# Two-operand SBUF instructions ahead of the up projection pinned to GpSimd, and a new instruction order

## The chip, the cores and the metric

The kernel runs on one core of a Trainium2 chip. The metric is device time in microseconds (us): the time before is the median of three runs. In the profile the engines are called PE (TensorE matmul), PEld (TensorE weight load, beside PE), DVE (VectorE), ACT (ScalarE), POOL (GpSimd) and SP (SyncE, which issues nearly all DMAs). Each engine works through its own list of instructions in order; semaphores hold an instruction until what it reads or overwrites is ready.

## The reference

One block of a network on x of 2048 tokens by 512 channels, in fp32, with six modulation rows (silu(c) times w_mod). First half: linear attention with 32 heads of 16 channels; second half: a token-shift mixer and an MLP with 1376 hidden channels.

```python
x = A_x
mod = (_silu(c) @ w_mod).reshape(c.shape[0], 6, 1, -1)
sa, ca, ga, sb, cb, gb = (mod[:, 0], mod[:, 1], mod[:, 2], mod[:, 3], mod[:, 4], mod[:, 5])
h = _layernorm(x, axis=-1) * (1 + ca) + sa
x = x + ga * _A_ref(h, A_wqkv, A_w_phi, A_wo)
h = _layernorm(x, axis=-1) * (1 + cb) + sb
x = x + gb * _B_ref(h, B_w1, B_w2, B_w3, B_w4)

# in _A_ref: per head, phi = (softmax(p), softmax(-p)) of p = q @ w_phi and of p = k @ w_phi
kv = jnp.einsum("bhsf,bhsd->bhfd", phi_k, v)
z  = jnp.einsum("bhsf->bhf", phi_k)
num = jnp.einsum("bhqf,bhfd->bhqd", phi_q, kv)
den = jnp.einsum("bhqf,bhf->bhq", phi_q, z)[..., None] + 1e-6
o = num / den

# in _B_ref: h = gelu(layernorm(x) @ w1), four channel quarters shifted by +1, -1, +2, -2 tokens
x1 = x + hs                                   # hs = shifted h @ w2
h2 = _gelu(_layernorm(x1, axis=-1) @ w3) @ w4  # the up projection is w3, the down projection w4
return x1 + h2
```

## The kernel before

Tokens are worked in 8 chunks of 256 (c) and in 16 tiles of 128 rows (t). A product of two fp32 operands is made of three fp32r matmuls on a high and a low part of each (`three`), so every operand is split: one instruction copies the high part, a second one subtracts it from the source to get the low part (`hi_lo`). That subtraction has two SBUF operands where the source lies in SBUF, and so has most of what this change touches.

The body does not issue instructions. It records about 2800 steps in a plan, each with an engine, the engines that could do it instead (`alts`), and what it reads and writes. At the end `emit` issues them in the order of the table ORDER: a list of step numbers, where a letter behind a number sends the step to another engine that it allows (A is ACT, V is DVE, G is POOL). SLOT gives the buffer of every tile of each kind. Both tables were found ahead of time by a planner that is not in the file. So the place of each instruction on its engine, and its buffer, are fixed numbers.

The stages, by the names of their groups in `plan.at` and of their tiles:

- `wk`, `wq`, `wv`: weights of the first half are folded or split (`bd`, `rk`, `raw`, tile `w`); `w1`, `w2`, `gb`: modulation rows are accumulated (`mod`, `acc`); `w3`: `wo` is scaled by ga and split; `w7`: w1 and w2 are split.
- `h`: layer norm of a chunk (`xl`, `xn`, transposed in `pt`, split into `hh`). `k`: key features `ke` of a tile (reductions `k`, exponentials, then `ke` times the reciprocal sums). `v`: `vv`. `kv`: 32 small matmuls into `kva`, and the sum of the features over tokens, `za`, plus `ke`. `q`: query features `qe`, by way of a copy `qt` for most tiles, and a store to DRAM.
- `phi`: features come back as `e`; `ez` is `e` times the column sums `z` of `za` (broadcast), reduced to the denominators `pz`. `tr`: `e` times the weights `q`, then a DVE transpose to `pT`. `num`: matmuls on `pT`, then `oT`. `o`, `n`: projection by wo, residual, two moments of layer norm (each with a POOL power `rs`), transposed and split to `nT`. `g`: w1, gelu into `gf`, split into `sh`. `sh`: small POOL copies of two columns between the `sh` of neighbouring chunks, for the shifts. `x`: the matmuls by w2 on `sh`.
- `w50` to `w54`: five parts of w3 (`wr`) are made into seven products each (`ws`: sums and differences, then splits) and stored to DRAM, since the up and down projections use a scheme with seven block products. `w40` to `w44`: w4, scaled by gb and split (`raw`, `tw`, `w`).
- `l`, `t`: layer norm of the second half and its block operands (`bL`, `tr`, `bH`). `u`: the up projection (PE tile `pa` from `bH` and the w3 products `wq`). `b`, `d`, `out`: the down projection (`ac` from `gg`) and the output.

Two-operand instructions are recorded by `tt`. Those that may run on DVE or POOL get POOL as an alternative, and ORDER decides for each one. In the profile a tile's trailing digits are cut off, so `k1` and `k2` both read `k`, and `q1` to `q5` read `q`; in the order lists below names end with a running number of the buffer.

Of the kernel before, what the change touches and what calls it, by code (L numbers as in the profile page):

```python
# [164 lines left out]
)  # L165
SLOT = {
    "pp": "510234426360573046405216574732325716511600313075732270653365216523706542035040435752736700267672"
          "4243153510404460571",
    "bd": "46",
    "w": "134625cd387165ad28cb09",  # L170
    "rk": "73958dgc",
# [195 lines left out]
def body(ctx: ExitStack, tc, x, wqk_t, wv_d, wo_d, w1_d, w2_d, w3_d, w4_d, c_d, wmod_d, id_d, cst_d, cst2_d, out):  # L367
# [308 lines left out]
    if BIAS["start"] > 1:  # L676
        plan.at("wq")
        wq = load_folded(0)
# [709 lines left out]
```

## Time and profile before

| | |
|---|---|
| median of 3 runs | 554.66 us (554.64 to 555.55) |
| the profiled execution | 554.69 us, of which the instructions span 552.9 us |
| PE busy | 544.9 us, 4498 matmuls |
| DVE busy | 488.6 us, 903 instructions |
| ACT busy | 351.7 us, 828 instructions |
| POOL busy | 344.5 us, 351 instructions |
| HBM | 89.74 MB read, 34.35 MB written |

How to read it: a view by windows gives the busy time of each engine in stretches of the span. A view of groups gives, for instructions of one line, engine and shape, count, total and mean time, and behind the second bar how long the engine had been idle before them and which engine and line ended most of that. A timeline row merges neighbouring instructions of one kind: start, length, engine, what, how many. The chain of work that ended last is followed back from the last instruction, at each step to what released it.

### The profile page before, as it was taken

Reading aid. Unit: us, or ns where it says so; the run is one execution under the profiler, and the core shown is the slowest. Engines: PE = TensorE matmul, PEld = TensorE weight load, DVE = VectorE, ACT = ScalarE, POOL = GpSimd, SP = SyncE. Lnnn points to the kernel's source line nnn. Section 1 sums busy time; section 2 is a strip of 40 time slices with the busy share of each in tenths; the row PEclk is TensorE's granted clock in tenths of the full one; section 3 lists DMA queues with packets and bytes.
Section 4 is the critical chain, followed back from the end, with each engine's and each line's share of the span. In section 5 each row is a group of like instructions: output and inputs, shape, how many; then the busy total and the mean of one; then the engine's idle time right before and its main releaser. Section 6 shows DMA issues by size and latency. Waiting matters only on the chain.

```text
span 552.9 us, 12370 instructions
## 1 busy us (share of the span) xinstructions
PE 544.9 (99%) x4498; PEld 488.1 (88%) x4498; DVE 488.6 (88%) x903; ACT 351.7 (64%) x828; POOL 344.5 (62%) x351
## 2 busy tenths in 40 slices
PE   8999999999989999999999999999999999999997
PEld 7888788878767788888889898999999999999996
DVE  3999999899999999999998878987888868896886
ACT  2899898834436788969888877866434543434540
POOL 2499985979599999978886545234150434254442
PEclk9999999999999999999999999999999999999999
DMA  8982544537736766869987878986689673872022
GB/s 323 392 277 89 175 170 137 176 112 248 205 118 226 249 195 206 275 235 319 292 275 270 242 257 301 339 356 231 284 248 347 245 284 97 264 286 80 25 92 95
DMA packets 63749, 124.90 MB, mean 226 GB/s; under 512 B 7140, under 2 KB 26852, under 8 KB 59592
## 3 DMA queue, kind: packets, MB, share of 16 engines
q1 hardware_dynamic: 63400, 124.04, 66.4%
q8 instruction: 35, 0.57, 0.4%
q14 instruction: 26, 0.21, 0.1%
q10 hardware_dynamic: 288, 0.07, 0.1%
HBM read 89.74 MB, written 34.35 MB: 224 GB/s over the span
## 4 chain that ended last, share of the span: by engine, by line
PE 86%; DVE 7%; POOL 3%; DMA 2%; issue 1%; ACT 0%; DVEq 0%; POOLq 0%
PE pp L471 36%; PE pa L471 27%; PE ac L471 20%; PE pt L480 2%; DVE pz L442 2%; DVE q L442 2%; DMA mod<-in_wmod 1%; PE kva L471 1%; POOL qe L420 1%; DVE pT L762 1%; POOL ez L420 1%; POOL e L420 1%; DVE ez L418 1%; DMA const<-in_c 1%; DVE pp L437 0%
## 5 line engine op out<-in xcount | busy, mean ns | idle before, releaser
L471 PE MATMUL pp<-w,hh 128*128 128x512 f32 x576 | 138.8, 397 | 0.0
L471 PEld LDWEIGHTS pp<-w,hh 128*128 128x128 f32 x576 | 106.7, 188 | 26.1 <-issue 1.6
L471 PE MATMUL pa<-bH,wq 128*128 128x256 f32 x840 | 106.7, 281 | 0.0
L471 PE MATMUL ac<-w,gg 128*128 128x256 f32 x840 | 106.6, 281 | 0.0
L471 PEld LDWEIGHTS ac<-w,gg 128*128 128x128 f32 x840 | 103.4, 189 | 1.1
L471 PEld LDWEIGHTS pa<-bH,wq 128*128 128x128 f32 x840 | 103.1, 189 | 0.9
L471 PE MATMUL pp<-w,sh 128*128 128x512 f32 x192 | 49.4, 399 | 0.0
L471 PE MATMUL pa<-nT,w 128*128 128x256 f32 x384 | 48.3, 282 | 0.8 <-DVE nT L418 0.7
L471 PEld LDWEIGHTS pa<-nT,w 128*128 128x128 f32 x384 | 46.8, 188 | 2.5 <-DVE nT L418 1.2
L471 PE MATMUL pp<-w,oT 128*128 128x512 f32 x192 | 47.4, 395 | 0.0
L471 PEld LDWEIGHTS pp<-w,oT 128*128 128x128 f32 x192 | 35.4, 188 | 8.1 <-DVE oT L418 0.7
L401 ACT ACTIVATE gg<-cu 128x256 fp32r<-128x256 f32 (+1 forms) x56 | 19.1, 359 | 35.1 <-PE ac L471 19.7
L471 PEld LDWEIGHTS pp<-w,sh 128*128 128x128 f32 x192 | 34.6, 188 | 7.5 <-issue 0.8
L588 POOL TENSOR_TENSOR rs<-mv,const 128x2 f32<-128x2 f32 x31 | 23.8, 769 | 25.3 <-ACT mv L595 23.7
L401 ACT ACTIVATE cu<-pa 128x512 f32<-128x512 f32 (+1 forms) x42 | 21.5, 519 | 27.6 <-PE pa L471 22.3
L420 POOL TENSOR_TENSOR gg<-cu,gg 128x128 fp32r<-128x128 f32 (+1 forms) x26 | 15.8, 615 | 33.2 <-ACT gg L401 13.9
L420 POOL TENSOR_TENSOR ez<-e,const 128x1024 f32<-128x1024 f32 x12 | 29.2, 2433 | 5.2 <-DMA dram<-qe 5.1
L401 ACT ACTIVATE gg<-sg 128x512 fp32r<-128x512 f32 x38 | 23.1, 624 | 14.0 <-POOL sg L420 6.0
L420 POOL TENSOR_TENSOR e<-e,q 128x1024 f32<-128x1024 f32 x15 | 28.8, 1938 | 0.4 <-DVE q L418 0.2
L418 DVE TENSOR_TENSOR gg<-cu,gg 128x256 fp32r<-128x256 f32 (+1 forms) x54 | 22.1, 416 | 7.6 <-PE ac L471 4.6
L418 DVE TENSOR_TENSOR gg<-sg,gg 128x512 fp32r<-128x512 f32 x36 | 26.0, 722 | 3.0 <-PE ac L471 1.5
L420 POOL TENSOR_TENSOR ke<-ke,k 128x1024 f32<-128x1024 f32 x14 | 27.2, 1952 | 1.2 <-DVE k L445 1.2
(214 smaller groups left out, 1211.5 us busy)
## 6 DMA issues: line engine op xcount, KB each, us to landing
wq<-dram SPq DMA_DIRECT2D x32, 1024.0 KB, 7.8
dram<-ws SPq DMA_DIRECT2D x35, 256.0 KB, 3.1
xl<-in_x SPq DMA_DIRECT2D x32, 256.0 KB, 4.1
dram<-qe SPq DMA_DIRECT2D x16, 512.0 KB, 3.7
e<-dram SPq DMA_DIRECT2D x64, 128.0 KB, 3.2
raw<-in_w SPq DMA_DIRECT2D x18, 256.0 KB, 3.7
mod<-in_wmod SPq DMA_DIRECT2D x16, 256.0 KB, 5.2
dram<-xl SPq DMA_DIRECT2D x16, 256.0 KB, 3.0
```

Source lines behind the costliest of these rows:

```text
L401: nc.scalar.activation(o(), i(), func, **kw)
L418: dve = ("DVE", 71 + 1.04 * o.n + 90 * (isps(a) and isps(b)), lambda: nc.vector.tensor_tensor(o(), a(), b(), op=op))
L420: pool = ("Pool", cost, lambda: nc.gpsimd.tensor_tensor(o(), a(), b(), op=op))
L442: plan.op("DVE", 65 + 1.04 * a.n + 110 * isps(o), lambda: nc.vector.tensor_reduce(o(), a(), axis=AX.X, op=op), [o], [a])
L471: nc.tensor.matmul(o(), a(), b(), start=s, stop=e, **kw)
L480: nc.tensor.transpose(o(), i(), ident())
L588: plan.op("Pool", 540 + 10 * m, lambda: nc.gpsimd.tensor_tensor(r(), v(), mhalf[:, :m](), op=OP.pow), [r], [v, mhalf])
L762: plan.op("DVE", 71 + 1.04 * o.n, lambda: nc.vector.transpose(o(), i()), [o], [i])
```

## The change

`tt` looks at the group of a step. In the groups `k`, `q`, `kv`, `w` (with digits: w0 to w7, w50 to w54 and w40, but not w41 to w44), `phi`, `tr`, `g`, `sh` and `gb`, a step that could run on either engine is recorded for POOL alone. Everything with an operand in PSUM stays on DVE, and so do the small instructions that had no alternative. The groups of the up and down projections keep their choice. ORDER and SLOT are replaced as a whole, so all engines run their work in a new order, the choices that are left (copies on ACT, DVE or POOL, and the free two-operand steps) are made anew, and tiles have other buffers. The file is three lines longer in all, and `tt`'s DVE instruction has line 417 in place of 418, its POOL instruction line 419 in place of 420.

```diff
 ORDER = (
-    "0 3 35 6 52 2 42 50 5 54 56 36 237 23 7 37 11 1 12 13 14 17G 31 10 38 86G 19 39 43 88 8 44 18 9 49V 84 27 40 "
...
+    "2744 2786 2702 2666 2785 2758 2667 2787 2668 2774 2700 2760 2788 2759 2789 2791G 2703 2771 2790 2775 2704 "
+    "2792G 2772 2793 2795 2794 2776 2796 2799 2797 2800 2798"
 )
 SLOT = {
...
-    "bd": "46",
+    "bd": "39",
...
         pool = ("Pool", cost, lambda: nc.gpsimd.tensor_tensor(o(), a(), b(), op=op))
         both = lock and (o.n >= 256 or eng != "DVE")
-        plan.op(*dve, [o], [a, b], alts=[pool] if both else [], lock=lock)
+        g = plan.group.rstrip("0123456789")
+        if both and g in ("k", "q", "kv", "w", "phi", "tr", "g", "sh", "gb") and plan.group not in ("w41", "w42", "w43", "w44"):
+            plan.op(*pool, [o], [a, b])
+        else:
+            plan.op(*dve, [o], [a, b], alts=[pool] if both else [], lock=lock)
```

The first place is on DVE, where the denominators of the first query tiles are made (`ez` is e times z, `pz` the reduction). Before:

```order
L418 TENSOR_TENSOR ke_1708<-ke_1708,k_340_1738 128x1024
L418 TENSOR_TENSOR w_1730<-raw_1436,w_1703 128x512
L418 TENSOR_TENSOR qe_1826<-qt_1755,q_345_1762 128x1024
L418 TENSOR_TENSOR w_1671<-raw_1295,w_1271 128x512
L418 TENSOR_TENSOR ez_1902<-e_1388,const_1853 128x1024
L418 TENSOR_TENSOR ez_1906<-e_1618,const_1853 128x1024
L442 TENSOR_REDUCE pz_1925<-ez_1902 128x64
```

and DVE at the same place now:

```order
L445 TENSOR_REDUCE q_343_1789<-qt_1781 128x32 x2
L409 TENSOR_SCALAR vv_1827<-pp_1792 128x512
L409 TENSOR_SCALAR const_1851<-pp_1822 128x256
L445 TENSOR_REDUCE pz_1893<-ez_1884 128x64
L445 TENSOR_REDUCE pz_1893<-ez_1891 128x64
L440 SCALAR_TENSOR_TENSOR pz_1893<-q_313_1530,pz_1893 128x64
```

Six two-operand instructions left DVE here, and two copies out of PSUM (`vv` and the column sums, `const`) came in from ACT.

The second place is POOL in the same part of the program: the last sums of keys, the first `ez`, the first `e`. Before:

```order
L420 TENSOR_TENSOR ke_1680<-ke_1680,k_339_1733 128x1024
L420 TENSOR_TENSOR za_800<-za_800,ke_1680 128x1024
L420 TENSOR_TENSOR ez_1908<-e_1782,const_1853 128x1024
L420 TENSOR_TENSOR w_1671<-raw_969,w_1271 128x512
L1007 MEMSET sh_1955 128x4x2
L420 TENSOR_TENSOR qe_1959<-qt_1910,q_368_1930 128x1024
L420 TENSOR_TENSOR e_1388<-e_1388,q_377_1966 128x1024
L420 TENSOR_TENSOR e_1618<-e_1618,q_377_1966 128x1024
```

and POOL now:

```order
L419 TENSOR_TENSOR za_791<-za_791,ke_1608 128x1024
L419 TENSOR_TENSOR ke_1716<-ke_1716,k_334_1742 128x1024
L419 TENSOR_TENSOR qe_1829<-qt_1781,q_343_1789 128x1024
L419 TENSOR_TENSOR ez_1884<-e_1221,const_1851 128x1024
L419 TENSOR_TENSOR ez_1891<-e_1524,const_1851 128x1024
L419 TENSOR_TENSOR w_1915<-raw_1430,w_1296 128x512
L419 TENSOR_TENSOR ez_1941<-e_1711,const_1851 128x1024
L419 TENSOR_TENSOR e_1221<-e_1221,q_371_1962 128x1024
L419 TENSOR_TENSOR qe_1990<-qt_1939,q_372_1964 128x1024
L419 TENSOR_TENSOR ez_2001<-e_1908,const_1851 128x1024
L419 TENSOR_TENSOR e_1524<-e_1524,q_371_1962 128x1024
```

All four first `ez` are on POOL now, and the second `e` is the 104th instruction of the plan on POOL where it was the 90th.

The third place is POOL at the column copy from the `sh` of chunk 3 into the `sh` of chunk 2 (a CAST, the last of the rows shown); the w2 matmuls of tile 5 (`x5`) read it. Before:

```order
L420 TENSOR_TENSOR sh_3316<-gf_3252,sh_3316 128x2x256
L420 TENSOR_TENSOR ws_3241<-ws_3241 128x256
L420 TENSOR_TENSOR ez_3419<-e_2781,const_1853 128x1024
L588 TENSOR_TENSOR rs_3455<-mv_3416,const_118 128x2
L1004 CAST sh_3085<-sh_3316 128x4x2
```

and now:

```order
L419 TENSOR_TENSOR sh_3355<-gf_3281,sh_3355 128x2x256
L419 TENSOR_TENSOR raw_1966<-raw_1966,gb_2524 128x512
L419 TENSOR_TENSOR w_3490<-raw_3104,w_3308 128x512
L591 TENSOR_TENSOR rs_3503<-mv_3438,const_67 128x2
L419 TENSOR_TENSOR e_2809<-e_2809,q_670_3497 128x1024
L419 TENSOR_TENSOR e_3087<-e_3087,q_670_3497 128x1024
L1007 CAST sh_3566<-sh_3355 128x4x2
L419 TENSOR_TENSOR tw_3571<-raw_1966 128x256
L1007 CAST sh_3238<-sh_3355 128x4x2
```

The copy was the 168th instruction of the plan on POOL and is the 196th now. Counted by kind, up to and with the copy: `za` 9 before and 14 now, `ez` 12 and 16, `ws` 34 and 45, `w` (subtractions of 512) 13 and 16, `raw` 3 and 6, `ke` 14 and 16, `e` 12 and 14, `sh` (subtractions) 6 and 8, `qe` 11 and 12, `acc` (additions) 11 and 12, `tw` 0 and 1; fewer are `acc` (scalings) 3 and 0, `bd` 4 and 2, `xn` 3 and 2, `mod` 2 and 1, `w` (copies) 2 and 1. The copies between chunks are 6 and 7; all other kinds are the same in number.

More of the change, by code (lines that the diff above doesn't have):

```diff
@@ L40 @@
 ORDER = (
[124 rows of a table removed]
[123 rows of a table added]
 )
 SLOT = {
-    "pp": "510234426360573046405216574732325716511600313075732270653365216523706542035040435752736700267672"
-          "4243153510404460571",
-    "bd": "46",
-    "w": "134625cd387165ad28cb09",
-    "rk": "73958dgc",
-    "xl": "01lif20gi5bh89hdfh4a36c0kejafg2h50eh36ecj9hl0aac",
-    "st": "03b8g32eh379c16aej5837hgb7h96dj2b",
-    "mv": "14fa06bdj2bdg379c16c68i2h9ie7064a",
-    "rs": "26hc17fi148hj2bdg34j2a19ef1c4f78e",
-    "nm": "57ei9dj54a89cg056afei0548fhi02bd54bd03aiaeg0fj581cg539hi",
@@ L177 @@
-    "xn": "ab75aj6ejag7f54b",
-    "mod": "ekbk73e1dj930hf2ke",
-    "mod2": "1023",
-    "kva": "4",
-    "za": "7",
-    "hh": "0789abe0",
-    "pt": "71713064136760724740255030200105",
-    "raw": "948hcla7b2l2g59fd34940abi351",
-    "k1": "0110502430210140",
-    "ke": "4501639451823940",
-    "k2": "5343025543253140",
-    "vv": "3246ekjhkfh0170l",
-    "qe": "7692282134682731",
-    "q1": "3242123515032015",
-    "qt": "ajj9ib759209",
-    "acc": "clf1e",
-    "kvs": "1",
-    "pz": "1",
@@ L195 @@
-    "q2": "03105351",
-    "e": "5617956458034928",
-    "ez": "4988322399990775",
-    "q3": "1245243214024032",
-    "q5": "44423145",
-    "pT": "3044399695373795",
-    "oT": "4a4ea04b",
-    "nT": "b05444be",
-    "n": "l12l4aaf1h5kje7g",
-    "h": "7519l62c7i1lfkcd",
-    "gf": "21535500",
-    "sh": "92be2cb0",
-    "pa": "720435033552357536277143075740636220453477601263027041460272",
-    "wr": "80061",
-    "ws": "010ie23c3782d1hgibgibgfbd0id69267k7",
-    "gb": "8",
-    "tw": "08935",
@@ L212 @@
-    "bL": "47604149",
-    "nb": "dgdj5dhj4gg4jbjd",
-    "yt": "9fje7gehj940707c",
-    "bH": "23820419431994595628147378657521",
-    "tr": "e10a2k3haldgbhd0",
-    "wq": "e90c934e174e3174e7314e7134e14317e431",
-    "cu": "672egi14hdfl25b7c1364hg9ked6l14g9cd0jblf",
-    "gl": "big235l6",
-    "ac": "26311637061227465013415304762351",
-    "gg": "25789138572584716831287609283795063284107962583265103241806937415809261809713458",
-    "sg": "kf6fka6k0j0k94h3la253c4b4acl7276ki2k97e4",
-    "xb": "9had9ei0fj3haf15",
@@ L224 @@
-    "xc": "5le904k6jhi2fg2i",
-    "uu": "00k2i6ck",
+    "pp": "261305532640421075722365757064416403320062054043536071021151535323725140237431473401270212137314"
+          "1455126707426232736",
+    "bd": "39",
+    "w": "124635ce7812d93eab4c61",
+    "rk": "6548agfd",
+    "xl": "01jk728f34250h629fjklc4b12fjf94005bejea995bfkik2",
+    "st": "04b8i57ah56fh12cej4653hd88e95i128",
+    "mv": "15fa03cej27ei56fh12d26iah9ge4jd7c",
+    "rs": "26gc16fg1acbj37di5a1ac09ehjf7g46e",
+    "nm": "37dh9ej4289dbi04389dg04a89bg037f478g13cbcbi0bj26f053a9hb",
@@ new lines @@
+    "xn": "bc530h2e8j1diflj",
+    "mod": "e41kbb6l7j0g1gcdfb",
+    "mod2": "0123",
+    "kva": "7",
+    "za": "6",
+    "hh": "0789abd0",
+    "pt": "17061432046516324014155271147117",
+    "raw": "adei5bec5ea38ilg9i4chl3g82j3",
+    "k1": "0115103053403512",
+    "ke": "4510832450897120",
+    "k2": "0245412514230503",
+    "vv": "jlagakic2kc0bk60",
+    "qe": "8692987557041279",
+    "q1": "3243210425301425",
+    "qt": "6c4dh60hdg4d",
+    "acc": "i9bl1",
+    "kvs": "k",
+    "pz": "6",
@@ new lines @@
+    "q2": "01431415",
+    "e": "3492856084157839",
+    "ez": "6166611591981242",
+    "q3": "2352052052302340",
+    "q5": "44310235",
+    "pT": "0666519698212482",
+    "oT": "94a04a4b",
+    "nT": "6b5645cb",
+    "n": "a0a0jajl6961f5cf",
+    "h": "h86eckda28kb61a0",
+    "gf": "73451854",
+    "sh": "93b5abc6",
+    "pa": "020450207004503750163642753457216043701622754731536201453626",
+    "wr": "71360",
+    "ws": "7c9dkh4f45h6905d30e36bhld39g5e4j81g",
+    "gb": "7",
+    "tw": "59618",
@@ new lines @@
+    "bL": "73075863",
+    "nb": "l9h5dii0ckki8lel",
+    "yt": "0f00ef59h9lh6dld",
+    "bH": "41597429841261092637406918177164",
+    "tr": "dh4lhajdiac08gj6",
+    "wq": "406407580278502785207850278027580752",
+    "cu": "edc3b4915hc8a6jhf3dik8cilba9f02gi384jh60",
+    "gl": "gb5e3c2g",
+    "ac": "02615612745373620147041723054172",
+    "gg": "65341526939852493682794617093417289350487215970297524906825790132485017235906481",
+    "sg": "6g60ai0g524le21de50ed65k8j0hfa9l5fag5lbf",
+    "xb": "f50k9bg241kde61k",
@@ L226 @@
+    "xc": "ejgelc4a1d0350ac",
+    "uu": "h45669i0",
 }
```

244 rows, old and new, of the table ORDER are left out of this document.

## Prediction

> **What bounds the kernel now.** I read the page first: the busy times, the slices and the chain that ended last.
>
> ```profile
> span 552.9 us, 12370 instructions
> ...
> PE 544.9 (99%) x4498; PEld 488.1 (88%) x4498; DVE 488.6 (88%) x903; ACT 351.7 (64%) x828; POOL 344.5 (62%) x351
> ...
> PE   8999999999989999999999999999999999999997
> ...
> POOL 2499985979599999978886545234150434254442
> ...
> PE 86%; DVE 7%; POOL 3%; DMA 2%; issue 1%; ACT 0%; DVEq 0%; POOLq 0%
> ```
>
> PE sets the time: it is idle for 8 us of the span, and four fifths of the chain are its matmuls. The change moves no matmul to or from PE, so it can help by little, and can hurt where another engine makes PE wait. POOL's 62% hide two halves: slices of 7 to 9 up to about 280 us, mostly 2 to 5 later. The edit puts work into the full half. So I went to windows, cut where the argument needs it.
>
> ```profile
> core 0: us, PE busy (x) PEld busy (x) DVE busy (x) ACT busy (x) POOL busy (x), PEclk, DMA share, GB/s
> 0.00:60.00 60.00, 58.30 (x340) 49.14 (x340) 50.23 (x90) 45.21 (x109) 41.34 (x46) 1.00 0.74 266
> 60.00:150.00 90.00, 90.00 (x864) 72.12 (x864) 86.12 (x112) 58.99 (x128) 71.06 (x46) 1.00 0.53 170
> 150.00:259.00 109.00, 106.48 (x954) 87.98 (x953) 106.62 (x180) 79.87 (x186) 100.48 (x81) 1.00 0.70 224
> 259.00:300.00 41.00, 41.00 (x367) 35.79 (x365) 39.51 (x68) 34.46 (x91) 34.27 (x37) 1.00 0.84 278
> ```
>
> Up to 259 us POOL works 41.34 + 71.06 + 100.48 = 212.9 us and idles 46.1: 18.7 in the first window, 18.9 in the second, 8.5 in the third. DVE is as full: 243 of 259.
>
> I cut at 259 because there POOL makes the column copy between the shifted tiles of chunks 2 and 3, which the w2 matmuls of tile 5 need (third place in the order lists).
>
> ```profile
> 259.04 0.19 POOL L1004 CAST sh<-sh 128x8 fp32r<-128x8 f32 x1
> 264.35 4.37 PE L471 MATMUL pp<-w,sh 128*128 128x512 f32 x18
> ```
>
> The copy ends at 259.2. PE's row of 18 matmuls holds tile 6 and tile 5 mixed, three matmuls a part; the first part that reads the copy starts about 0.5 us into it. In the new PE order some 1.3 us of other matmuls come ahead of it, so PE would reach it at about 266. Slack: about 7 us. I tried the same subtraction at earlier points (last `ke` for the sums, first `e`, the fourth chunk's) and it comes out later and later as POOL's list goes on; this copy is where it is worst.
>
> **The change, part by part.**
>
> *Work put on POOL ahead of the copy.* Counts are from the order lists, durations from these groups:
>
> ```profile
> ...
> L420 POOL TENSOR_TENSOR za<-za,ke 128x1024 f32<-128x1024 f32 x8 | 19.3, 2413 | 4.3 <-DVE za L418 4.3
> L420 POOL TENSOR_TENSOR ez<-e,const 128x1024 f32<-128x1024 f32 x12 | 29.2, 2433 | 5.2 <-DMA dram<-qe 5.1
> L420 POOL TENSOR_TENSOR ws<-ws 128x256 fp32r<-128x256 f32 x14 | 10.5, 756 | 4.0 <-ACT ws L401 3.9
> L420 POOL TENSOR_TENSOR w<-raw,w 128x512 fp32r<-128x512 f32 x13 | 17.9, 1375 | 0.1
> L420 POOL TENSOR_TENSOR raw<-raw,acc 128x512 f32<-128x512 f32 x2 | 2.6, 1288 | 0.0
> L420 POOL TENSOR_TENSOR ke<-ke,k 128x1024 f32<-128x1024 f32 x14 | 27.2, 1952 | 1.2 <-DVE k L445 1.2
> L420 POOL TENSOR_TENSOR e<-e,q 128x1024 f32<-128x1024 f32 x15 | 28.8, 1938 | 0.4 <-DVE q L418 0.2
> L420 POOL TENSOR_TENSOR sh<-gf,sh 128x512 fp32r<-128x512 f32 x11 | 12.2, 1121 | 3.8 <-DVE sh L410 3.6 <-ACT nm L595 0.2
> L420 POOL TENSOR_TENSOR qe<-qt,q 128x1024 f32<-128x1024 f32 x11 | 22.4, 2036 | 3.3 <-DVE pz L437 2.5 <-DVE q L442 0.8
> L410 POOL TENSOR_SCALAR acc<-mod,const 128x512 f32<-128x512 f32 x3 | 2.1, 696 | 0.8 <-ACT xn L401 0.8
> L420 POOL TENSOR_TENSOR bd<-const 128x128 f32<-128x128 f32 x4 | 1.7, 454 | 4.5 <-DMA const<-in_cst 4.5
> ```
>
> Added: 5 `za` 12.1; 4 `ez` 9.7; 11 `ws` at 0.75, 8.2; 3 `w` 4.1; 3 `raw` and 1 `acc`, of the same size, 5.2; 2 `ke` 3.9; 2 `e` 3.9; 2 `sh` 2.2; 1 `qe` 2.0; 1 `tw`, 256 wide as `ws`, 0.8. Together 52.1 us. Gone: 3 scalings of `acc` 2.1; 2 `bd` 0.9; three copies of 512 elements like the scalings, 2.1. Net: 47 us, so POOL has 212.9 + 47 = 260 us of work up to the copy.
>
> *How much idle time stays.* Were there none, the copy would end at 260. The idle time of the first 60 us is waiting for loads and the first features:
>
> ```profile
> POOL w L410 <- DMA raw<-in_wv: 7.8, 1, 7.8
> POOL bd L420 <- DMA const<-in_cst: 4.5, 1, 4.5
> POOL za L420 <- DVE za L418: 4.3, 2, 2.6
> POOL ez L420 <- DMA dram<-qe: 5.1, 1, 5.1
> POOL rs L588 <- ACT mv L595: 9.0, 5, 3.2
> PE pp L471 <- DVE pT L762: 1.7, 1, 1.7
> ```
>
> The first two are of that kind, and DVE and PE have the same work up to there, so I keep 18.7 and add one for the first `qe`, which has less POOL work ahead of it now: 20. The next two are POOL out of work, waiting for its turn in a sum that DVE shared, or for the first reloaded features. With `za` all its own and a backlog of tens of us these go. The ends are none of the 27.4 us after 60 us, and half of it (the `rs` row, waits on moments from ACT, may recur in any order). I take none: from the thirteenth slice to the seventeenth (166 to 235 us), where POOL had a backlog before too, its slices read 9.
>
> *The sum.* 260 + 20 = 280 us for the copy, against 266 for PE: 14 late. In the overlap with DVE, POOL's rows get longer:
>
> ```profile
> 145.46 2.82 POOL L420 TENSOR_TENSOR ez<-e,const 128x1024 f32<-128x1024 f32 x1 [5.13 <-DMA dram<-qe]
> 148.24 2.30 POOL L420 TENSOR_TENSOR w<-raw,w 128x512 fp32r<-128x512 f32 x1
> 255.66 2.40 POOL L420 TENSOR_TENSOR ez<-e,const 128x1024 f32<-128x1024 f32 x1
> 31.91 1.28 POOL L420 TENSOR_TENSOR w<-raw,w 128x512 fp32r<-128x512 f32 x1
> 145.95 3.42 DVE ez L418
> ```
>
> The same `ez` and `w` took 2.82 and 2.30 beside DVE's two `ez` (3.42), 2.40 and 1.28 elsewhere: 1.4 us more. DVE's `ez` are gone, so I take 1 off: 13 late. Were all of POOL's 260 us 2% shorter for lack of such company, it would be 5 off, 9 late; without the us for the first `qe`, 8: the lower end. The upper end, with half of the later idle time kept, is 28.
>
> The Trainium skill, in Advanced Engine Details and Errata, VectorE Performance Modes, says that DVE's second SBUF port is shared with GpSimd and that two-port DVE instructions and GpSimd block each other. By that rule the edit takes away one side of the quarrel, and the sum would be 9 late, 564 us, where the group means give 13 and 568. The five rows agree with it.
>
> The wait builds up rather than falling on one matmul: the column sums need the last `ke`, then the first `num` the second `e` (104th on POOL, 90th before), then the shifts. Behind each, PE's whole list is queued. After the copy POOL's list goes on at a pace below PE's (34.27 of 41 us busy before), so the distance closes. I keep 13 us to the end, since nothing on PE can be made up: 58.3 of 60, 90 of 90, 41 of 41.
>
> *What else moves.* DVE loses about as many instructions of 0.7 to 1.8 us as POOL gains, some 34 us, and takes about 20 copies out of PSUM from ACT, 14 us: free, since PE waits for POOL then. SP's list carries the stores of `ws` in their new places; the last that counts for the up projection's third product is 43 POOL instructions, 38 us, behind the copy: 280 + 38 = 318, then
>
> ```profile
> dram<-ws SPq DMA_DIRECT2D x35, 256.0 KB, 3.1
> wq<-dram SPq DMA_DIRECT2D x32, 1024.0 KB, 7.8
> ```
>
> so 329 us. By its place in PE's list of matmuls, PE comes to that product at about 330 without delay and 343 with it: hidden, with some 13 us over; if SP were held up longer than that, the rest would be added one for one. The start (PE waits for the same loads) and the tail (down projection, not pinned) I cost at nothing, within 1 us each way. The profiled execution is 554.69 us, its span 552.9, the median of the runs 554.66. So 552.9 + 13 = 566 for the span and 554.7 + 13 = **568 us** for the time.
>
> **Rivals.**
>
> *POOL's cover holds, no change* (553.6 to 555.7). POOL had 46.1 us idle before the copy and gets 47; with all of it used and 7 us of slack, PE would not wait. Against it: 18.7 of the idle us lie where there is nothing to do yet. It decides at 13 us of 260, that is POOL 5% faster than its rows; no group above has that much to give.
>
> *DVE was the brake, faster.* The chain runs through DVE and POOL for much of 144 to 204 us, and PE loses time there:
>
> ```profile
> 154.00:168.00 14.00, 12.28 (x131) 9.37 (x120) 13.86 (x21) 6.05 (x12) 13.90 (x8) 1.00 0.41 132
> ```
>
> With two `ez` and other work off DVE, the 1.7 us of PE idle (the wait for `pT` above) could go: 554.7 - 1.7 = 553. It decides if POOL has the `e` for that `pT` done by then; but POOL is busy 13.90 of 14 here, as full as DVE, with more work ahead of that `e` now.
>
> *POOL waits too, much slower.* PE, held up by POOL, hands `o` and `n` to POOL's powers (`rs`) later, and POOL's list is in order, so it stands behind them with the `ez` of later tiles: the two engines then wait in turns. Half of 27.4 us of idle time comes back: 554.7 + 28 = 583 at the end, 576 to 590. For it: 9.0 us of waits of `rs` on ACT before; against it, they were where POOL had run dry.
>
> *The clock.* The 1.7 us above are PE's longest idle time between 12 and 549 us, and the clock stayed full.
>
> ```profile
> 549.00:551.00 2.00, 0.08 (x1) 0.00 (x0) 0.75 (x2) 0.00 (x0) 0.00 (x0) 1.00 0.55 183
> 551.00:552.90 1.90, 0.00 (x0) 0.00 (x0) 0.00 (x0) 0.00 (x0) 0.00 (x0) 0.57 0.18 65
> ```
>
> At the end it falls to 0.57 two us after the last matmul. If the 13 us come as three or four waits of over 2 us, each could be followed by a slow stretch, a microsecond or two; most of that would be taken out of the next wait for POOL, and only behind the last does it count: 570. TensorE: Matmul & The Clock Gate, Part 1, of the Trainium skill, puts the idle window and the time to recover at about 3.4 us each, half clock between; by it one such wait costs an estimated 1.7 us, the same 570.
>
> **How the numbers follow.** Two kernels are told apart from about 0.2%, 1.1 us. POOL sets the pace and PE ends 8 to 21 us late: 0.70, 562 to 576, likeliest 568; in 0.15 of this the clock falls behind the last wait (570). Less than 8 but over 1.1 us: 0.08. Waiting in turns, over 576: 0.14. No change 0.03, faster 0.05. So slower 0.92. From 560 to 579 there lies the first case, about half of the second and a third of the third: 0.8.
>
> **What would show it.** Right: POOL's slices read 9 from the third to about the twentieth; its busy time goes from 344 to about 390 us; PE idle, in waits of some us between 140 and 270 us, put down to POOL's `ke`, `e` or `sh` or DVE's `pT` behind them; POOL's share of the chain far above 3%; the copy at about 280; DVE's busy time lower and its idle time larger; from 300 us on all as before. Wrong: POOL idle for more than 25 us up to the copy (in turns), POOL's means shorter by 4% or more (the cover holds), or PE's waits put down to loads by SP.

## Result and the profile after

The changed kernel takes 564.98 us (median of four runs, 564.34 to 565.49), the kernel before beside it 554.88 us: 1.018 times as long, 95% interval 1.0167 to 1.0194. That is 10 us slower. The profiled execution took 564.34 us.

First the page of the changed kernel: the busy times, POOL's slices and the chain that ended last.

```profile
span 562.6 us, 12352 instructions
...
PE 549.2 (98%) x4498; PEld 488.0 (87%) x4498; DVE 478.1 (85%) x896; ACT 341.9 (61%) x811; POOL 379.9 (68%) x375
...
POOL 1499999999999999999997844625140323423422
...
PE 58%; DVE 2%; issue 0%; DVEq 0%
```

POOL gained 35 us, DVE lost 10.5 and ACT 10. POOL's slices are full from the third to the twenty-first, as the forecast had it. The chain shows no POOL, but its shares add up to only 60%: its first piece starts at 218.3 us, so it is silent on all that came earlier. The same windows as before:

```profile
0.00:60.00 60.00, 58.13 (x342) 47.77 (x342) 51.52 (x92) 46.81 (x110) 39.37 (x41) 1.00 0.78 280
60.00:150.00 90.00, 88.97 (x856) 71.24 (x853) 74.58 (x102) 52.16 (x116) 90.00 (x61) 1.00 0.44 140
150.00:259.00 109.00, 103.13 (x921) 83.56 (x920) 99.66 (x165) 71.73 (x163) 109.00 (x85) 0.98 0.72 221
259.00:300.00 41.00, 41.00 (x332) 33.71 (x331) 37.84 (x67) 33.72 (x91) 38.74 (x40) 1.00 0.85 280
```

POOL idles for 20.6 us in the first window and then not once up to 259 us. PE is full again from 259 on: what it loses, it loses before, most of it in the third window (5.9 idle there against 2.5 before). The column copy of the forecast and PE's rows around it:

```profile
274.65 0.21 POOL L1007 CAST sh<-sh 128x8 fp32r<-128x8 f32 x1
```

```profile
274.80 0.67 PE L474 MATMUL pp<-pT,const 64*32 64x128 f32 x32
275.39 2.36 PE L474 MATMUL pp<-w,sh 128*128 128x512 f32 x9
```

The copy ends at 274.9, and the parts that need it start at 275.39, close behind, yet in an unbroken run of matmuls. So nothing is waited for there. PE's longest waits, from the list of waits:

```profile
PE pa L474 <- ACT nT L400: 2.1, 1, 2.1
PE pp L474 <- DVE pT L765: 1.7, 1, 1.7
PE pp L474 <- POOL ke L419: 1.0, 1, 1.0
```

The wait for `pT` is the one of before; the other two are new. How late PE is at a place is read from rows of the same matmuls. Ahead of the last three places PE has done the same matmuls in both kernels; ahead of the first the changed kernel has done 32 small ones more, about 0.6 us of work. The places are the column sums of `ke`, the first `num` of chunk 1 (I call it num1), the first product by w1 (g0, which some expectations below call the up projection's first), and `num` of chunk 2 (num2). Before, then after:

```profile
143.13 0.61 PE L471 MATMUL pp<-ke,const 128*32 128x256 f32 x8
174.86 0.67 PE L471 MATMUL pp<-pT,const 64*32 64x128 f32 x32
188.76 0.28 PE L471 MATMUL pa<-nT,w 128*128 128x256 f32 x1
192.66 1.16 PE L471 MATMUL pp<-pT,const 64*32 64x128 f32 x64
```

```profile
145.80 0.64 PE L474 MATMUL pp<-ke,const 128*32 128x256 f32 x8 [1.03 <-POOL ke L419]
177.80 0.67 PE L474 MATMUL pp<-pT,const 64*32 64x128 f32 x32
194.59 0.38 PE L474 MATMUL pa<-nT,w 128*128 128x256 f32 x1 [2.08 <-ACT nT L400]
195.31 4.51 PE L474 MATMUL pa<-nT,w 128*128 128x256 f32 x23 [0.34 <-DVE nT L417]
199.75 1.16 PE L474 MATMUL pp<-pT,const 64*32 64x128 f32 x64
```

PE is 2.7 us late at the column sums, 2.9 at num1, 5.8 at g0, 7.1 at num2. The spans differ by 9.7. So seven of the ten us are lost by 200 us, and four of them between num1 and num2. In that stretch 23 matmuls took 4.51 us, where they take 2.98 in a run below: the clock was at half rate from 195.4 for 3.4 us.

### The profile page after: what moved, and what is told of

The parts are those of the page before. It is cut to its first block, busy times and chain, and to the rows that moved or that the text cites. A ratio compares the mean times of both kernels' runs of the same rounds, so it can differ in the third digit from the quotient of the medians.

```text
span 562.6 us, 12352 instructions
## 1 busy us (share of the span) xinstructions
PE 549.2 (98%) x4498; PEld 488.0 (87%) x4498; DVE 478.1 (85%) x896; ACT 341.9 (61%) x811; POOL 379.9 (68%) x375
## 4 chain that ended last, share of the span: by engine, by line
PE 58%; DVE 2%; issue 0%; DVEq 0%
PE pa L474 26%; PE ac L474 20%; PE pp L474 12%; PE pt L483 1%; DVE q L445 0%; DVE pT L765 0%; DVE pp L440 0%; DVE pz L445 0%; DVE oT L417 0%; DVE h L440 0%; DVE nT L409 0%; DVE pz L448 0%; DVE q L417 0%; DVE xb L417 0%; DVEq L1387 0%
## 5 line engine op out<-in xcount | busy, mean ns | idle before, releaser
L474 PE MATMUL pa<-nT,w 128*128 128x256 f32 x384 | 49.7, 288 | 2.7 <-ACT nT L400 2.1
L474 PEld LDWEIGHTS pa<-nT,w 128*128 128x128 f32 x384 | 48.0, 194 | 4.4 <-ACT nT L400 2.3
L419 POOL TENSOR_TENSOR ez<-e,const 128x1024 f32<-128x1024 f32 x16 | 38.9, 2446 | 0.0
L417 DVE TENSOR_TENSOR gg<-sg,gg 128x512 fp32r<-128x512 f32 x40 | 27.8, 698 | 7.3 <-ACT gg L400 4.8
L419 POOL TENSOR_TENSOR w<-raw,w 128x512 fp32r<-128x512 f32 (+3 forms) x21 | 25.6, 1221 | 11.8 <-DVE w L409 9.3
L400 ACT ACTIVATE cu<-pa 128x512 f32<-128x512 f32 (+1 forms) x37 | 18.8, 515 | 23.6 <-PE pa L474 22.8
L400 ACT ACTIVATE gg<-sg 128x512 fp32r<-128x512 f32 x35 | 21.4, 622 | 17.2 <-DVE sg L417 10.1
L419 POOL TENSOR_TENSOR e<-e,q 128x1024 f32<-128x1024 f32 x16 | 31.5, 1975 | 0.0
L419 POOL TENSOR_TENSOR za<-za,ke 128x1024 f32<-128x1024 f32 x13 | 31.2, 2399 | 0.0
L419 POOL TENSOR_TENSOR ke<-ke,k 128x1024 f32<-128x1024 f32 x16 | 31.0, 1940 | 0.0
```

Of the source, the lines that this page charges most:

```text
L400: nc.scalar.activation(o(), i(), func, **kw)
L417: dve = ("DVE", 71 + 1.04 * o.n + 90 * (isps(a) and isps(b)), lambda: nc.vector.tensor_tensor(o(), a(), b(), op=op))
L419: pool = ("Pool", cost, lambda: nc.gpsimd.tensor_tensor(o(), a(), b(), op=op))
L474: nc.tensor.matmul(o(), a(), b(), start=s, stop=e, **kw)
```

## Experiments

All times are medians beside the kernel before on the same chip (554.8 to 555.1 us). The forecast's theory, A below, says that POOL's work ahead of the copy sets the time, one for one.

### One part undone: the engines back, the order kept

All 42 steps that the kernel before had on DVE go back to it, in the new order.

```diff
-            plan.op(*pool, [o], [a, b])
+            plan.op(*pool, [o], [a, b], alts=[dve])
...
+            if o.i in BACK:
+                o.fn = o.alts["DVE"][1]
```

> The new order and buffers are kept, but the 42 pinned steps that ran on DVE before run on DVE again, each at its place in the new order. Theory A (GpSimd's load sets the pace): GpSimd's work up to the column copy for tile 5 falls from 254 to about 215 us, the copy ends before 262 us, PE's waits of 186 to 215 us go, time 553.5 to 557. Theory B (the new order itself, on DVE, ACT and the DMA queue, is the slow part): GpSimd's load falls as much, but the time stays at 563 to 566.

Measured: 582.82 us, ratio 1.0473 (1.0416 to 1.0529). No theory had it slower than the change. DVE's list in the new order has no room for these steps: in this kernel's window from 60 to 150 us DVE is as good as full, and PE idles 4 us there and 10 in the next.

```profile
60.00:150.00 90.00, 85.96 (x764) 67.55 (x762) 88.36 (x118) 50.89 (x115) 62.82 (x42) 1.00 0.38 117
150.00:259.00 109.00, 99.01 (x914) 78.89 (x912) 100.50 (x158) 66.71 (x147) 95.28 (x71) 0.97 0.69 209
```

The new order is made for the new engines. It cannot be judged with the old ones, so this run says nothing on A.

### The other part alone: pinned, in the old order

The kernel before with the rule on engines, its list of orders and places kept.

```diff
-        plan.op(*dve, [o], [a, b], alts=[pool] if both else [], lock=lock)
+        g = plan.group.rstrip("0123456789")
+        if both and g in ("k", "q", "kv", "w", "phi", "tr", "g", "sh", "gb") and plan.group not in ("w41", "w42", "w43", "w44"):
+            plan.op(*pool, [o], [a, b])
+        else:
+            plan.op(*dve, [o], [a, b], alts=[pool] if both else [], lock=lock)
```

> The old order and buffers are kept, and only the rule is applied: every step that the rule names runs on GpSimd, at its old place. Theory A: GpSimd has about 41 us more up to the column copy, is busy without a break from about 35 us on, and PE waits: 564 to 575, no better than the new order since the old places were not chosen for it. Theory B: without the new order the loss is gone, 554 to 557.

Measured: 569.70 us, ratio 1.0250 (1.0215 to 1.0285), in A's range. Pinning alone costs 14.6 us, and the new order takes about 4.5 of them back. PE's rows show where:

```profile
149.86 0.64 PE L475 MATMUL pp<-za,const 128*32 128x256 f32 x8 [1.04 <-POOL za L420]
153.00 1.08 PE L475 MATMUL pp<-ke,const 128*32 128x256 f32 x8 [2.50 <-POOL ke L420]
186.42 0.67 PE L475 MATMUL pp<-pT,const 64*32 64x128 f32 x32
205.08 1.16 PE L475 MATMUL pp<-pT,const 64*32 64x128 f32 x64
```

Against before PE is 9.9 us late at the column sums, with both waits on POOL, 11.6 at num1 and 12.4 at num2. Here the loss comes ahead of num1. The changed kernel is only 2.9 late there and loses 4.2 between the two. In this run alone PE also waits for a column copy of POOL, for 1.0 us at 263 us.

### Work handed to DVE, and work doubled

Two runs that shift POOL's load ahead of the column sums by a few us: seven `ws` steps on DVE, and the same seven issued twice on POOL.

```diff
+BACK = {770, 771, 772, 773, 787, 790, 793}
...
+            if o.i in BACK:
+                o.fn = o.alts["DVE"][1]
```

```diff
+TWICE = {770, 771, 772, 773, 787, 790, 793}
...
             yield o
+            if o.i in TWICE:
+                yield o
```

> As the changed kernel, but seven instructions of the first part of w3 (256 elements each, the first quarter of the span) run on DVE. Theory A: 4.9 us less on GpSimd, so the column copy ends near 269.8 in place of 274.6 and the time falls by about that, to 560 to 561 (slope 1 as long as PE still waits). Theory B: DVE has 2.5 us more and nothing else moves, 565 to 567.

> As the changed kernel, but the same seven instructions are issued twice on GpSimd (the second writes the same values again). Theory A: 4.9 us more on GpSimd, the column copy ends near 279.5, time 569 to 570.5. Theory B: GpSimd is not what PE waits for, 564.5 to 566.

Measured: on DVE 568.28 us (1.0223, 1.0182 to 1.0264), doubled 572.81 us (1.0301, 1.0265 to 1.0337). The doubling went A's way, but by 7.8 us for 5.0 us of work; PE's start at num2, 207.52 us, is 7.8 us later as well. The first went against every theory: POOL relieved, and the kernel 3.3 us slower. Its rows on POOL and on DVE show what it met, with a `ws` on DVE from the run with the engines back, when POOL was idle, as a third:

```profile
77.15 2.40 POOL L422 TENSOR_TENSOR za<-za,ke 128x1024 f32<-128x1024 f32 x1
```

```profile
77.72 2.11 DVE L420 TENSOR_TENSOR ws<-wr 128x256 f32<-128x256 f32 x1
```

```profile
98.12 0.41 DVE L422 TENSOR_TENSOR ws<-wr,ws 128x256 fp32r<-128x256 f32 x1
```

An instruction with two SBUF operands that can take 0.41 us on DVE took 2.11: it starts under POOL's `za` and ends at 79.83, 0.28 us behind it. A second of the seven did the same (2.03 us, ending 0.29 behind a `za`). What DVE does for PE stands behind it in its list, and a few us later PE waits 2.4 us for DVE's `hh`, with the clock at half rate for 3.4 us around the end of that wait. The Trainium skill, in Advanced Engine Details and Errata, GPSIMD Details, says that POOL shares a read and a write interface with DVE and conflicts with DVE instructions on two SBUF inputs; these rows agree with it.

### POOL relieved, DVE spared

The mirror of the doubling: steps on POOL that work in place are left out, and DVE gets nothing.

```diff
+SKIP = {775, 778, 781, 784, 883, 886, 889, 892}          # and 211, 297, 299, 393 in the second
...
-            yield o
+            if o.i not in SKIP:
+                yield o
```

> The changed kernel with eight of POOL's in-place subtractions left out, the low parts of ws of w50 and w51 (775, 778, 781, 784, 883, 886, 889, 892), so that those low parts are not formed. It is the run with seven doubled turned round: POOL alone is relieved, and DVE gets nothing. They took 0.73 us each in the changed kernel and 0.70 from start to start, so POOL's work up to the copy falls from 254.0 by 5.7 to 248.3 us. Theory A (POOL's work ahead of the copy sets the time, one for one): the copy ends at 268 to 270 instead of 274.9 and the time falls from 565.0 by 4 to 6, to 559-561 us. Theory B (the new order costs PE its time through DVE or ACT, and POOL's added work is mostly hidden): 563-566 us.

> The same with four more of POOL's steps left out, the sums za of four tiles (211, 297, 299, 393) at 2.40 us each: 15.3 us less for POOL than in the changed kernel, all of it ahead of the column sums, and nothing more for DVE. Theory A: the copy could end at 259 to 261, ahead of PE's arrival at 266, so nearly all of the loss is gone: 554-557 us. Theory B: what POOL does not set remains, 562 us or more. Theory C (half is POOL, half is the way DVE and ACT stand in the new order): 558-561 us.

Measured: 563.61 us (1.0161, 1.0147 to 1.0175) and 563.33 us (1.0156, 1.0142 to 1.0170). A is refuted as I had put it: 5.7 and 15.3 us less for POOL gave 1.4 and 1.7 us, not 4 to 6 and 8 to 11. In the second run POOL has next to no lead to show for it; the first row is the changed kernel's:

```profile
134.55 1.94 POOL L419 TENSOR_TENSOR ke<-ke,k 128x1024 f32<-128x1024 f32 x1
...
134.44 1.94 POOL L421 TENSOR_TENSOR ke<-ke,k 128x1024 f32<-128x1024 f32 x1 [0.87 <-DVE k L450]
142.43 1.94 POOL L421 TENSOR_TENSOR ke<-ke,k 128x1024 f32<-128x1024 f32 x1
194.58 2.04 POOL L421 TENSOR_TENSOR e<-e,q 128x1024 f32<-128x1024 f32 x1
```

It runs dry several times up to 134 us, the last three times waiting for DVE's `k` (1.2, 0.2 and 0.9 us), which comes when PE and DVE get to it. So with 15.3 us less to do, POOL starts the `ke` at 134.4 only 0.1 us earlier. From there on its list runs without a gap past num2. Two of the `ws` left out, 1.4 us, stand behind this place, ahead of the last `ke`: and the last `ke` ends at 144.4 instead of 145.8, PE's wait of 1 us at the column sums is gone, and num2 starts 1.3 us earlier, at 198.44. What was left out ahead of 134 us gave nothing; these two steps counted in full.

### The half clock, first attempt, and DVE relieved in the kernel before

To fill PE's wait at g0, 17 more matmuls were put ahead of operation 761, one of the two products of g0. In PE's list it is the second of them, so the filling came behind the wait, at a place where PE had no time to spare.

```diff
+            if marks["w1", c].i == 761:
+                def fill(p=p, real=marks["w1", c].fn):
+                    for _ in range(17):
+                        nc.tensor.matmul(p[:, 0, :](), w1[0][:, 0, 0:P](), w1[0][:, 0, 0:CH](), start=True, stop=True)
+                    real()
+                marks["w1", c].fn = fill
```

> The changed kernel with 17 further matmuls of 128x256 on PE, into the same tile of PSUM just ahead of the first product of the up projection's first tile, which overwrites them: nothing is left out. They fill PE's wait of 2.08 us for nT at 192.5 us, behind which 23 matmuls ran at half clock and took 4.51 us instead of 2.8 to 3.0. Theory A (the drop of the clock only takes the place of a wait that POOL's copy would bring at 275 us): no stretch at half clock near 195, PE waits about 1 us at the copy instead, and the time is 564-565 us, within 1 of the changed kernel's 565.0. Rival (the drop is a cost of its own): 563.0-563.6 us, the 1.6 us given back to the end.

Measured: 566.87 us, ratio 1.0215 (1.0198 to 1.0231). The wait of 2.08 us and the half clock are as they were, so nothing is tested of what was meant.

```profile
201.02 2.30 PE L972 MATMUL pa<-w 128*128 128x256 f32 x17
```

It does say that 2.3 us of work for PE behind g0 cost 1.9: POOL's copy, some 75 us later, absorbs next to none of it.

This run has the changed kernel's lists up to num2, and its chain of work reaches back to 146 us. From 176 to 190 us the chain is POOL's list, one instruction behind the other; then it goes on like this:

```profile
189.27 0.70 POOL rs L591
190.51 1.53 ACT n L400 x2
195.54 4.46 PE pa L474 x23
```

The moments `rs` of chunk 0 let ACT make `n`; PE transposes it, the transposes are copied to `nT`, and g0 waits for that. In the kernel before and in the changed one the same `rs` stands here:

```profile
183.93 0.69 POOL L588 TENSOR_TENSOR rs<-mv,const 128x2 f32<-128x2 f32 x1
```

```profile
189.01 0.73 POOL L591 TENSOR_TENSOR rs<-mv,const 128x2 f32<-128x2 f32 x1
```

It is 5.1 us later, and g0 is 5.8 later.

The other run is the kernel before with 17 in-place steps of DVE left out, those that the change gave to POOL:

```diff
+SKIP = {211, 297, 299, 315, 393, 401, 405, 508, 539, 647, 775, 778, 784, 886, 1106, 1213, 1320}
```

> The kernel before, in its own order, with 17 in-place steps left out that it had on DVE and that the change gave to POOL (five za, two ke, six ws, two raw, one acc, one e; 16.7 us on DVE, 14.3 of it ahead of the copy). POOL and PE get nothing new. It is the half of the change that takes work from DVE, alone. Theory A (DVE was no brake in the kernel before; PE is 99% busy): 553.8-555.5 us, within 1 of its own 555. Rival (DVE was the brake at the wait for pT of 1.7 us): 552.5-553.7 us.

Measured: 555.01 us, ratio 1.0005 (0.9996 to 1.0014). DVE was no brake in the kernel before: with 16.7 us less of its work the wait of 1.72 us for `pT` stays.

### The order at g0 and POOL's late work

Four runs: two edits one by one, both together, and both with the twelve early steps left out as well. The wait at g0 stands right behind the transposes of `n0`, since the new order moved a block of `o2` ahead of them; the first edit puts it back behind them.

```diff
-... 826 752 821 1119 757 1011 753 758 827 754 985 ... 755 776 1015 1005 830 832 918 756 759 822 760 831 ... 765
+... 752 821 1119 757 1011 753 758 754 826 985 ... 755 776 1015 1005 918 756 759 822 760 827 830 832 831 ... 765
```

The second leaves out nine late steps of POOL.

```diff
+SKIP = {990, 993, 996, 999, 1097, 1100, 1103, 1485, 1487}
```

> The changed kernel with one block of six matmuls of 512 columns (operation 826, o2) moved in PE's list back to where the kernel before has it: behind n0's transposes and ahead of the first product of the up projection, which reads what they give. The DVE and ACT operations that read the block (827, 830, 832) move behind the copies of nT with it. Nothing is left out. PE would so have 1.5 us of work in its wait of 2.08 us for nT at 192.5 us. Theory A (POOL's copy at 274.9 us sets the end, and what PE loses ahead of it only shortens its wait there): the half clock behind that wait goes, PE then waits 2 to 3 us at the copy, and the time is 563.8-565.2 us. Theory D (the wait and the half clock behind it are costs of the new order by themselves, 1.5 + 1.7 us): 561.5-562.5 us.

> The changed kernel with nine in-place steps of POOL between 223 and 267 us left out, seven low parts of ws (w52 and w53, 0.77 us each) and two scalings of raw by gb (1.33 us each): 8.0 us less for POOL, all of it behind the column sums, where POOL ran without a gap from 134 to 273 us in the runs with steps left out ahead of them. Their results are not formed. Theory A (POOL's copy sets the end): the copy at 266-268 us; PE by its own losses up to 212 us reaches it at 273.5, so the time falls by 1.5 to 2.5 only, to 562.5-563.5 us. Theory D (POOL's load does not matter any more, PE's losses up to 212 us are all): 564.5-565.5 us.

> Both edits together: the six matmuls moved back and the nine steps left out. Theory A: the copy is off PE's way (266-268 against PE at about 270-271) and the wait and the half clock at 192-198 us are gone, so both give what neither gives alone: 560-562 us. Theory D: as the moved block alone, 561.5-562.5; if the moved block does nothing, as the nine steps alone, 562.5-563.5 us.

> Both edits, and the twelve steps left out ahead of the column sums as well (eight low parts of ws and four za, 15.3 us): 23 us less for POOL. PE's loss of 1.1 us at the column sums goes too, and what then stays of the change is the wait for the second e, 1.7 us, which the kernel before has as well: 557-559.5 us if POOL's work is what costs. If a part of the loss lies with how DVE and ACT stand in the new order, 560 us or more.

| run | us | ratio, 95% interval |
|---|---|---|
| block moved back | 565.05 | 1.0180 (1.0164 to 1.0195) |
| nine late steps left out | 564.48 | 1.0187 (1.0162 to 1.0212) |
| both | 566.28 | 1.0201 (1.0185 to 1.0217) |
| both, and the twelve early steps | 563.22 | 1.0150 (1.0134 to 1.0165) |

The late steps are worth nothing: POOL then waits for others ahead of the copy, and the copy ends at 275.0, as late as with them.

```profile
259.67 0.69 POOL L593 TENSOR_TENSOR rs<-mv,const 128x2 f32<-128x2 f32 x1 [1.12 <-ACT mv L600]
268.58 0.69 POOL L593 TENSOR_TENSOR rs<-mv,const 128x2 f32<-128x2 f32 x1 [1.48 <-ACT mv L600]
274.78 0.20 POOL L1009 CAST sh<-sh 128x8 fp32r<-128x8 f32 x1
```

In the last run 23 us are gone and the copy still ends at 273.5. So in these runs the copy follows PE's lateness, which reaches POOL by way of the moments `mv`; it does not make it. In the changed kernel POOL works up to the copy without a gap, and is done half a us before PE comes.

The moved block has A's number with another cause. Its rows on PE, on DVE and on POOL:

```profile
191.85 1.36 PE L481 MATMUL pt<-const,n 128*128 128x128 f32 x8 [2.03 <-ACT n L398]
195.26 2.98 PE L472 MATMUL pa<-nT,w 128*128 128x256 f32 x23 [0.48 <-DVE nT L415]
199.96 1.16 PE L472 MATMUL pp<-pT,const 64*32 64x128 f32 x64 [1.72 <-DVE pT L763]
201.04 4.64 PE L472 MATMUL pa<-nT,w 128*128 128x256 f32 x24
```

```profile
198.66 1.25 DVE L763 STREAM_TRANSPOSE pT<-e 128x1024 f32<-128x1024 f32 x1
```

```profile
196.60 2.02 POOL L417 TENSOR_TENSOR e<-e,q 128x1024 f32<-128x1024 f32 x1
```

The 23 matmuls take 2.98 us again, but num2 starts no earlier: PE now waits 1.72 us for the `pT` that DVE makes of POOL's second `e` as soon as that ends at 198.62. So POOL's list reaches PE in two places close together, by `rs` at g0 and by this `e` at num2. In the changed kernel the first holds PE longer: `pT` is ready at 199.25, and PE comes at 199.75. Without the wait at g0 the second holds it until about the same time, 199.96. There the time is set, 75 us ahead of the copy. In the changed kernel and in the one before, POOL's stretch looks like this. The first row of each pair is the last `ke` ahead of the column sums, on DVE before and on POOL after; the second is the second `e` of num2.

```profile
141.02 1.22 DVE L418 TENSOR_TENSOR ke<-ke,k 128x1024 f32<-128x1024 f32 x1
187.62 3.83 POOL L420 TENSOR_TENSOR e<-e,q 128x1024 f32<-128x1024 f32 x2
...
142.26:191.45 49.19, 46.81 (x462) 36.05 (x461) 48.32 (x73) 26.50 (x57) 43.38 (x27) 1.00 0.64 201
```

```profile
143.81 1.94 POOL L419 TENSOR_TENSOR ke<-ke,k 128x1024 f32<-128x1024 f32 x1
145.70 2.03 POOL L419 TENSOR_TENSOR qe<-qt,q 128x1024 f32<-128x1024 f32 x1
195.94 1.99 POOL L419 TENSOR_TENSOR e<-e,q 128x1024 f32<-128x1024 f32 x1
...
145.76:197.93 52.17, 46.89 (x417) 36.18 (x418) 43.45 (x70) 26.85 (x59) 52.17 (x32) 0.98 0.65 203
```

Before, POOL works 43.4 us of 49.2 between the two. After, it has 8.8 us more and works without a gap, 52.2 us. So the second `e` is 6.5 us later: 3.5 by the later `ke` and 3.0 by the stretch. Num2 is 7.1 later. With the twelve early steps left out the same stretch is 52.2 us again, by the rows above from 144.4 to 196.6. That is why no relief ahead of it or behind it showed.

That the time is set by num2 shows in all the profiles. From the start of num2 to the end of the span it is 360.2 us in the kernel before and 362.8 in the changed one; in the ten other runs that pin the steps it lies between 362.8 and 364.2, whether they took 563 or 573 us. That POOL's list from 134 us to there sets num2 is shown by the runs for work ahead of it, for work behind it, and for the two `ws` inside it. The 8.8 us themselves, which the change put between the last `ke` and the second `e`, were not taken out by themselves: but for `e`, which `pT` is made of, no step there works in place and could be left out.

In these runs the half clock is not a cost of its own. In its profiled execution the run with both edits never had it before the end, and it was not faster:

```profile
201.04 3.10 PE L474 MATMUL pa<-nT,w 128*128 128x256 f32 x24
...
211.89 0.28 PE L474 MATMUL pa<-nT,w 128*128 128x256 f32 x1
```

Its 24 matmuls took 3.10 us where those of the moved block alone, at half clock, took 4.64. But it then waits 0.62 us for `oT`, and other waits follow: ten us later PE starts the next products by w1 at 211.89, and with the moved block alone at 211.97. The 1.2 us between the two runs' medians lie within their ranges (564.03 to 565.64, 564.90 to 567.07).

## Why the prediction was right, and where its reasons failed

- **The number.** 568 forecast, 564.98 measured, in the range and in the first case. The lower figure of the sum, 564 by shorter rows on POOL, was nearer than the one taken, but the rows were not shorter (next but one). In part the number is luck: the lateness was worked out for the copy, 9 us by its measured time (274.9 against 266), and PE lost 9.7 elsewhere. The two are near each other because the same list of POOL, without a gap, stands ahead of both places.
- **The idle time.** 20 us kept, 20.6 measured, and none of the later idle time came back: exact. (The 21 us that close the first case are not worked out in the forecast; its sum with half of the later idle time gives 28.)
- **The added work: the term that was mis-sized.** 47 us added, so 260 up to the copy. By the windows POOL works 274.9 - 20.6 = 254.2: 41 us added. The 6 us are overlap: the last `ke` is shown with 1.94 us, but the next instruction starts 1.89 behind it. Added up, POOL's rows up to the copy come to 218.7 us before and 266.2 after, 47.5 more, as forecast; with overlaps counted once, 213.1 and 254.2. Over all kinds the rows kept their length, though DVE's two-operand work was gone: what `w` and `rs` lost, `e`, `qe`, `ws` and others gained. So neither the us taken off for shorter rows nor the 5 of the lower figure came that way. The Trainium skill, in Perfetto Trace Analysis, GPSIMD Engine Instruction, advises to time POOL's instructions by the distance of their starts; that agrees with these rows.
- **The copy as the place where it decides: the step that failed.** Under "The sum" POOL's time for the copy was set against PE's, 280 against 266, and the difference kept to the end. The copy came at 274.9, near the sum, and nothing waits for it. With 8 and 23 us less for POOL it came at 275.0 and 273.5. Had the sum been right as a cause, the run with the early and late steps left out would have been as fast as before. What held in its place: POOL's sum has to be started where POOL last has to wait for an input once the work ahead is taken away. That is the `ke` at 134.4, whose `k` comes from PE and DVE, and the sum decides at g0 and num2. The second `e` ends at 145.8 + 52.2 = 198, `pT` 1.3 later; PE, held at g0 by `rs`, starts num2 at 199.75.
- **The build-up.** The forecast had PE late at the column sums, the first `num`, then the shifts. It came at the column sums (2.7 by there, of which 0.6 is work brought forward), at g0 and num2 (4.2 more by there than at num1), and not at the shifts.
- **After the copy.** "I keep 13 us to the end": PE keeps all it lost, and to the 7.1 us at num2 another 2.6 come up to the end of the span, in small pieces that no run took apart: at matmuls ahead of which both kernels have done the same, it is 7.8 late by 202 us of the kernel before, 8.9 by 260 and at the last matmul; 0.8 come behind that.
- **DVE was the brake, faster.** Refuted by the run that relieved DVE alone, 555.01 us.
- **POOL's cover holds.** Refuted: it needed nearly all of POOL's idle time, and 20.6 us of it stayed unused.
- **POOL waits in turns.** The coupling is real: most of what POOL is relieved of comes back as idle time (20.6 us up to the copy, 40 in the last run). But it did not make the kernel slower beyond the first case.
- **The clock.** The drop came where the rival had it, behind a wait of 2.08 us, and cost less than its 1.7 us, since it went into the next wait. TensorE: Matmul & The Clock Gate, Part 1, of the Trainium skill, has a window of about 3.4 us that runs freely. The stretch lasted 3.4 us, and two kernels with the same waits (2.03, 0.48 and 1.72 us; 1.99, 0.48 and 1.74) had one and none: the traces agree. The idle window of 3.4 us that the prediction cites from there did not stand ahead of the drop: in the 3.4 us up to 195.4 PE was busy for 0.99, so less idle time was enough here.
- **What would show it.** POOL's slices and DVE's and ACT's shorter times came as said; POOL's busy time is 380 for about 390, the copy 275 for 280; POOL's share of the chain, said to be far above 3%, is none, but that chain starts at 218 us and can't tell. DVE's busy time fell by 10.5 us, half of what the prediction's figures for it come to (34 gone, 14 added).
- **Costed at nothing.** The stores by SP showed no wait; the tail is 0.8 of the 2.6 us.

## What to carry to other kernels

To move work onto an engine with idle time, do not sum its list from the start to a late deadline. Take work away early in its list and see where the engine then last waits for an input; from there sum to the next results that PE takes from it. In this kernel idle time outside that stretch was no reserve, and work taken away outside it gave nothing back. An instruction that ends just ahead of its reader, as the copy did, may be following rather than leading; leave some work out ahead of it and see whether it moves.

## What the hardware showed

- A 128x256 instruction on two SBUF operands on DVE took 2.11 us instead of 0.41 when it started under a 2.4 us instruction of POOL on two SBUF operands, and ended 0.28 us behind it; a second took 2.03 and ended 0.29 behind. POOL's row did not grow. Seven steps moved from POOL to DVE, these two among them, made the kernel 3.3 us slower.
- PE's half clock came in pieces of 3.4 us, in the runs with the engines back, with the old order and with steps doubled also of 6.8 us. The pieces at g0 followed a wait of about 2 us, and the run with steps doubled had the same wait of 2.08 us there with full clock behind it.
